# Linear attention and a two-layer feed-forward: the second chunk's attention built like the later chunks' (block transposes, keys in two layouts)

## The chip, the cores and the metric

The kernel runs on one core of one Trainium2 chip. The metric is the device time of one execution in microseconds (us). An execution is compared with others of the same program on the same kind of chip; of the kernel before, three timed runs are shown, and one more execution was recorded by the hardware profiler.

## What is computed

The reference takes q, k and v of shape (8 batches, 8 heads, 576 positions, 64 features). q gets a softmax over its 64 features, k a softmax over the 576 positions. Then k^T v is formed for each head (a 64 x 64 matrix) and q is multiplied by it. The result, 4608 tokens of 512 features, goes through a feed-forward network with 2048 hidden units and a clipped quadratic as its activation.

```python
q_s = np.exp(q - np.max(q, axis=-1, keepdims=True))
q_s = q_s / (np.sum(q_s, axis=-1, keepdims=True) + 1e-09)
k_s = np.exp(k - np.max(k, axis=2, keepdims=True))
k_s = k_s / (np.sum(k_s, axis=2, keepdims=True) + 1e-09)
kv = np.einsum('bhsd,bhse->bhde', k_s, v)
x = np.einsum('bhsd,bhde->bhse', q_s, kv)      # then (tokens, 512)
...
h = x @ w_in
g = np.where(h >= 1, h, np.where(h <= -1, 0.0, (h + 1) ** 2 / 4))
out = g @ w_out
```

All arrays are float32, except the weights, which arrive as 64-bit words.

## The kernel before

**Tiling.** The 4608 tokens are nine chunks of T = 512. The 512 features are four pairs of heads (128 partitions each), the 2048 hidden units 16 blocks f of 128. Chunk 0 starts the kernel; chunks 0, 1 and 2 run the plain feed-forward; chunks 3 to 8 run in couples with fewer products. Every large product is a sum of three products of 128x128 by 128x512 in a reduced float32 format, because each operand is kept as a high and a low part. In the first layer of a plain chunk (`first_layer`, matmuls on line 1352) a block f takes four entries of three matmuls, one for each pair of heads; in the second (`second_layer`, line 1565) it takes four entries of three, one for each slice of 128 tokens. Chunk 0 uses the pairs in the order 0, 2, 1, 3 of the stored weights, so its first two entries of a block need only the first two pairs.

**Weights.** While chunk 0 runs, `weights` turns the 64-bit words into high and low parts: a load of 512 KB (line 496), a scale on ScalarE (503), a shift and a join on VectorE (508, 511), the high part by ScalarE (534), the low part by GpSimd (538). Each block has two halves: half 0 for the first layer, half 1 for the second. The half-0 weights are also stored to DRAM for later chunks (line 567). Four staging tiles (two tags of two) hold the words, so a load waits until an earlier half in its place is finished. Below, "half 1 of block 1" is `weights(1, 1)`.

**Attention, first form** (`attention`, lines 803 to 998, used for chunks 0 and 1 before). For each pair of heads: the keys come transposed (features on partitions, 288 KB), so the maximum over positions is one reduction along a row (853), and the exponential yields the sums (857). Then TensorE transposes the keys back, four blocks of 128 (line 864) and a tail of 64 (line 873), two copies bring them out of PSUM (432, 434), and k^T v is 10 products, which show as 20 matmul records (line 889). For q (256 KB, rows of tokens): maximum, subtract, exponential, sum, reciprocal and multiply, then four TensorE transposes (line 936) and a copy.

**Attention, second form** (`attention_two`, lines 1079 to 1300, used for chunks 2 to 8 before). Two pairs are handled together. The keys come twice, transposed (288 KB, for the maxima alone, line 1116) and in rows of positions (320 KB); v is 325 KB. The maxima are turned by VectorE (1122), stored to DRAM in two pieces and read back spread over all partitions (128 KB, `m_load`); then VectorE subtracts (1143), ScalarE takes the exponential (1149), and k^T v of both pairs is one group of 40 matmul records (line 1159). q comes in a layout of 32 x 32 blocks, so the maximum and the sum are completed with eight small copies and two combinations across blocks (lines 1251 and 1252), and the transpose is one VectorE instruction per pair (line 1287). TensorE does no transposes here.

After either form `x_two` multiplies q by k^T v for two pairs (line 739) and writes the high part (ScalarE, 754) and the low part (VectorE, 761) of x.

**Order.** Each helper above adds entries to a plan; no engine chooses at run time. The list `SEQUENCE` names the entries, by the number in which they were added, in the order in which they are issued, for all engines together; each engine runs its own entries strictly in that order. `SECOND` names the entries that go to their second engine (a copy on VectorE for ScalarE, a square on GpSimd for ScalarE). All DMAs are issued by SyncE (SP) in list order onto one queue. Numbers used below, as the code adds them after the change: 38 to 42 are the x of chunk 0's first two pairs (38 its matmuls, 39 and 41 the high parts, 40 and 42 the low parts), 81 to 85 the same for its other two pairs; 86 to 105 the weights of block 0 half 0, block 1 half 0 and block 0 half 1; 106 to 109 the first layer of block 0; 119 to 125 the half 0 of block 2 (121 its shift, 122 its join); 126 to 131 the half 1 of block 1 (126 its load, 128 its shift, 129 its join); 132 to 135 the first layer of block 1; 110 to 112 the clipping of block 0 (112 its last step, on VectorE); 145 to 151 the half 0 of block 3 (148 its join); 301 to 337 the attention of the second chunk's first two pairs.

Of the kernel before, what the change touches and what calls it, by code (L numbers as in the profile page):

```python
# [18 lines left out]
P = 128  # L19
# [40 lines left out]
KT = 2  # L60


QT, QB = 2, 32
# [32 lines left out]
class Ring:  # L96
# [289 lines left out]
def tile_linear_attention_then_ffn(  # L386
# [416 lines left out]
    def attention(c, pr, due, step, slack):  # L803

        n = f"{c}_{pr}"
        first = c == 0  # L810
        after = 0.0 if first else START
        t = {}
# [1004 lines left out]
```

## Time and profile before

| what | us |
|---|---|
| median of the three timed runs | 833.61 (831.25 to 834.84) |
| the profiled execution, whole | 833.62 |
| its span, first to last instruction | 831.5 |
| TensorE (PE) busy within the span | 821.9 |
| VectorE (DVE) / ScalarE (ACT) / GpSimd (POOL) busy | 511.3 / 400.7 / 298.5 |
| first matmul of the feed-forward (line 1352) starts | 21.09 |
| first matmul of the second layer (line 1565) starts | 29.09 |
| matmul record of line 1352 for chunk 1's first block | 119.00 |

The whole profiled execution is 2.1 us longer than its span. Matmul records overlap one another, since matmuls are pipelined: what a group costs is read from the starts of what stands before and behind it, not from its length. "Waited for" rows name the last thing that an idle engine waited for.

### The profile page before, as it was taken

The page shows a single profiled execution, that of the slowest core. Times are in us where ns is not written, and L with a number is a line of the kernel's source. Part 1 is how long each engine was busy: PE and PEld are TensorE (multiplying, and loading weights), DVE is VectorE, ACT ScalarE, POOL GpSimd, SP SyncE. Part 2 cuts the span into 40 slices and gives each one's busy share as a digit, 9 for nine tenths or more (in the row PEclk, how much of TensorE's full clock was granted, in tenths as well). Part 3 has the DMA queues.
Part 4 walks back from the last instruction along what each step waited for, and adds up shares of the span by engine and source line. Part 5 has one row for each costly group of instructions (what it writes and reads, how often), then busy time and mean ns, then how long its engine had stood idle before and what let it go on. Part 6 is the DMA issues. An engine that isn't in the chain of part 4 may idle for free.

```text
span 831.5 us, 12315 instructions
## 1 busy us (share of the span) xinstructions
PE 821.9 (99%) x4316; PEld 659.2 (79%) x4316; DVE 511.3 (61%) x948; ACT 400.7 (48%) x691; POOL 298.5 (36%) x264
## 2 busy tenths in 40 slices
PE   8999999999999999999999999999999999999998
PEld 6677778877777788877877888787778888788886
DVE  7867688677686867867687546656564144443311
ACT  6877656335365356535455435443453243444521
POOL 4655465453435373311433342323344301111021
PEclk9999999999999999999999999999999999999999
DMA  9897868667687667886867336465564245444232
GB/s 340 276 326 259 311 226 269 211 222 264 222 305 241 210 234 276 277 270 222 302 204 257 115 134 203 152 225 193 177 206 174 76 165 163 141 152 152 76 102 88
DMA packets 70957, 175.05 MB, mean 211 GB/s; under 512 B 8048, under 2 KB 9840, under 8 KB 70896
## 3 DMA queue, kind: packets, MB, share of 16 engines
q1 hardware_dynamic: 70896, 174.27, 62.3%
q8 instruction: 34, 0.56, 0.3%
q14 instruction: 27, 0.22, 0.1%
HBM read 130.71 MB, written 43.53 MB: 210 GB/s over the span
## 4 chain that ended last, share of the span: by engine, by line
PE 92%; DMA 3%; DVE 2%; POOL 1%; issue 1%; ACT 1%; SPq 1%; POOLq 0%; DVEq 0%; ACTq 0%
PE o L1565 45%; PE hA L1411 16%; PE h L1352 14%; PE hC L1411 8%; PE hb L1411 4%; DMA st<-in_w 3%; PE x L739 2%; PE kv L1159 2%; POOL wl L538 1%; SPq L831 1%; PE kv L889 0%; DVE st L508 0%; POOL q L916 0%; DVE st L511 0%; PE tp L936 0%
## 5 line engine op out<-in xcount | busy, mean ns | idle before, releaser
L1565 PE MATMUL o<-wl,gh 128*128 128x512 f32 x576 | 227.2, 394 | 1.0 <-issue 1.0
L1565 PE MATMUL o<-wh,gl 128*128 128x512 f32 x576 | 224.5, 390 | 0.2 <-DVE gl L1554 0.2
L1565 PE MATMUL o<-wh,gh 128*128 128x512 f32 x576 | 224.3, 389 | 0.0
L1411 PE MATMUL hA<-x,w 128*128 128x512 f32 x576 | 143.2, 390 | 0.0
L1508 POOL TENSOR_TENSOR r<-r 128x512 f32<-128x512 f32 x59 | 62.8, 1065 | 221.0 <-ACT r L1502 212.3
L1565 PEld LDWEIGHTS o<-wl,gh 128*128 128x128 f32 x576 | 108.1, 188 | 28.4 <-issue 4.3
L1411 PEld LDWEIGHTS hA<-x,w 128*128 128x128 f32 x576 | 107.8, 188 | 24.4 <-DVE c L1435 1.0
L1565 PEld LDWEIGHTS o<-wh,gl 128*128 128x128 f32 x576 | 108.1, 188 | 23.9 <-DVE gl L1554 1.2
L1565 PEld LDWEIGHTS o<-wh,gh 128*128 128x128 f32 x576 | 108.2, 188 | 21.7
L1352 PE MATMUL h<-x,w 128*128 128x512 f32 x432 | 109.3, 393 | 0.3 <-DVE x L761 0.2
L1352 PEld LDWEIGHTS h<-x,w 128*128 128x128 f32 x432 | 79.9, 188 | 20.1 <-DVE x L761 1.9
L1411 PE MATMUL hC<-x,w 128*128 128x512 f32 x288 | 74.3, 393 | 0.0
L1411 PEld LDWEIGHTS hC<-x,w 128*128 128x128 f32 x288 | 53.4, 188 | 14.2 <-ACT sn_P L432 2.9
L1549 ACT CAST gh<-gs 128x512 fp32r<-128x512 f32 x42 | 26.2, 623 | 78.2 <-PE o L1565 71.2
L1554 POOL TENSOR_TENSOR gl<-gs,gh 128x512 fp32r<-128x512 f32 x22 | 28.4, 1290 | 92.8 <-ACT gh L1549 87.6
L1502 ACT ACTIVATE r<-c,half 128x512 f32<-128x512 f32 x48 | 34.6, 722 | 47.4 <-DVE c L1435 45.8
L1502 ACT ACTIVATE r<-h,half 128x512 f32<-128x512 f32 x48 | 32.9, 688 | 44.6 <-PE h L1352 44.6
L1506 ACT ACTIVATE r<-r 128x512 f32<-128x512 f32 x85 | 53.3, 631 | 1.9
L1260 POOL TENSOR_TENSOR q<-q,qzb 128x512 f32<-128x512 f32 x28 | 32.6, 1182 | 54.1 <-DVE qzb L1282 52.2
L1511 DVE SCALAR_TENSOR_TENSOR h<-h,r 128x512 f32<-128x512 f32 x48 | 33.2, 694 | 28.6 <-ACT r L1506 17.6
L1554 DVE TENSOR_TENSOR gl<-gs,gh 128x512 fp32r<-128x512 f32 x20 | 14.6, 729 | 57.6 <-ACT gh L1549 56.1
L1511 DVE SCALAR_TENSOR_TENSOR c<-c,r 128x512 f32<-128x512 f32 x48 | 34.0, 714 | 12.8 <-ACT r L1506 8.7
(130 smaller groups left out, 1180.0 us busy)
## 6 DMA issues: line engine op xcount, KB each, us to landing
w<-b SPq DMA_DIRECT2D x50, 512.0 KB
w<-s SPq DMA_DIRECT2D x48, 512.0 KB
st<-in_w SPq DMA_DIRECT2D x32, 512.0 KB
g<-c SPq DMA_DIRECT2D x42, 256.0 KB
gs<-g SPq DMA_DIRECT2D x42, 256.0 KB
v<-in_v SPq DMA_DIRECT2D x32, 325.0 KB
q<-in_q SPq DMA_DIRECT2D x36, 256.0 KB
out<-osb SPq DMA_DIRECT2D x35, 256.0 KB
```

Of the source, the lines that this page charges most:

```text
L739: nc.tensor.matmul(t[r][cols, :, p0:p1], kvt[rows, g % NKV, pr, :], q[pr]["tq"][rows, :, p0:p1], start=True, stop=True, tile_position=(r * ...
L1159: nc.tensor.matmul(kv[d, i, :], t[pr]["k"][:, j, d], t[pr]["v"][:, j, e * (D + 1) : (e + 1) * (D + 1)], start=(j == 0), stop=(j == KJ - 1) ...
L1260: nc.gpsimd.tensor_tensor(qf, qf, at, alu)
L1352: nc.tensor.matmul(t["h"], lhs, rhs, start=(turn == 0 and i == 0), stop=(turn == NPAIR - 1 and i == 2),)
L1411: nc.tensor.matmul(banks[b]["h"], lhs, rhs, start=(begins and not kk and not m), stop=(ends and kk == 1 and m == 2), skip_group_check=True,)
L1502: nc.scalar.activation(t["r"], t["h"], AF.Relu, bias=half[:, :1], scale=0.5)
L1506: nc.scalar.activation(t["r"], t["r"], AF.Square)
L1508: nc.gpsimd.tensor_tensor(t["r"], t["r"], t["r"], ALU.mult)
L1511: nc.vector.scalar_tensor_tensor(t["h"], t["h"], 1.0, t["r"], ALU.max, ALU.min)
L1549: nc.scalar.copy(t["gh"], t["h"])
L1554: eng.tensor_tensor(t["gl"], t["h"], f32(t["gh"]), ALU.subtract)
L1565: nc.tensor.matmul(outs[c, j], lhs[:, s], rhs, start=(begins and i == 0), stop=(closes and i == 2),)
```

## The change

Chunk 1 is built by `attention_two` in place of `attention`; `attention` serves chunk 0 alone and loses the branches for other chunks. The host sends the row layout of the keys for one batch more (KT from 2 to 1) and the block layout of q for one chunk more (QT from 2 to 1). The second chunk's two halves take their keys through the "k" tiles. Both lists are new from the first entry to the last: the order of all 3234 entries (3240 before) and the choice of second engines.

```diff
-KT = 2
+KT = 1
-QT, QB = 2, 32
+QT, QB = 1, 32
...
 SEQUENCE = (
...
+    1, 0, 19, 20, 86, 44, 45, 310, 43, 11, 100, 2, 12, 3, 63, 93, 4, 22, 62, 21, 30, 23, 6, 321,
+    5, 31, 322, 7, 24, 25, 119, 8, 64, 26, 88, 313, 54, 27, 32, 55, 13, 33, 87, 14, 56, 15, 34,
+    16, 46, 57, 47, 35, 17, 18, 49, 48, 36, 102, 9, 58, 37, 89, 59, 50, 10, 51, 90, 95, 52, 73,
+    94, 60, 74, 53, 65, 61, 28, 96, 91, 66, 29, 101, 67, 68, 126, 97, 103, 92, 75, 98, 38, 323,
+    69, 76, 104, 77, 145, 120, 70, 301, 78, 324, 71, 99, 39, 121, 79, 72, 303, 128, 80, 105, 40,
+    41, 122, 106, 152, 123, 81, 42, 127, 325, 107, 132, 129, 82, 133, 84, 326, 146, 83, 130,
+    124, 85, 108, 302, 328, 109, 327, 171, 134, 309, 110, 125, 147, 135, 111, 131, 330, 329,
...
-    def attention(c, pr, due, step, slack):
+    def attention(pr, due, step):
...
+        lk = load("kt", kt[0, pr], [P, 1, S], 288)
+        lq = load("q", q[c, pr], [P, NJ, P], 256)
+        lv = load("v", v[c, pr], [P, KJ, P + 2], 325, wait=3.0)
...
-        if not first:
-            rpk.free(kc)
-            tr = do("PE", 0.25, 2.7, kt_tr2, ke, *rpk.wait())
-            tr.mode = 3
-            rk.free(tr)
...
-            tag = ("k", "st1")[h]
+            tag = "st1" if c > 1 and h else "k"
...
-    banks = (ps_a, "b"), (ps_a, "a")
-    one, two = (attend(1, h, START + STEP * (1 + 6 * h), STEP, 1.0, banks) for h in range(2))
-    next(one)
-    at((0, 4), one, two)
+    one, two = (attention_two(1, h, START + 8 + 24 * h, START + 26 + 24 * h) for h in range(2))
+    at((0, 3), one)
+    at((0, 4), one)
+    at((0, 5), two)
     at((0, 6), two)
```

The lines of the list shown are its first seven. In it the loads stand in this order: q and k of pairs 0 and 1, half 0 of block 0 (86), q and v of pair 2, v of the second chunk's pair 0 (310), k of pair 2, half 1 of block 0 (100), v of pair 0, q of pair 3, half 0 of block 1 (93), k of pair 3, v of pair 1, q of the second chunk's pairs 0 and 1 (321, 322), half 0 of block 2 (119), v of pair 3, v of the second chunk's pair 1 (313), half 1 of block 1 (126).

More of the change, by code (lines that the diff above doesn't have):

```diff
@@ L801, in x_two @@
             rxo.free(xdone[c, kk])
-    def attention(c, pr, due, step, slack):
-        n = f"{c}_{pr}"
-        first = c == 0
-        after = 0.0 if first else START
+    def attention(pr, due, step):
+        c, n = 0, f"0_{pr}"
         t = {}
@@ L818, in do @@
             return op(
-                engine, us, at(stage), emit, deps, port=port, slack=slack, after=after, other=other
+                engine, us, at(stage), emit, deps, port=port, other=other
             )
@@ L824, in emit @@
                 size = shape[1] * shape[2]
-                room = KJ * P if name == "k" else VROOM if name == "v" else size
-                if first:
-                    flat = e1.tile([P, room], F32, tag=f"{name}{pr}", name=f"{name}_{n}")
-                else:
-                    flat = ld.tile([P, room], F32, tag=name, name=f"{name}_{n}")
+                room = VROOM if name == "v" else size
+                flat = e1.tile([P, room], F32, tag=f"{name}{pr}", name=f"{name}_{n}")
                 t[name] = flat[:, :size].rearrange("p (j d) -> p j d", j=shape[1])
                 nc.sync.dma_start(t[name].rearrange("p j d -> p (j d)"), src)
-            r = ring(f"ld {name}{first}", NPAIR if first else NLOAD)
-            o = op("SP", 0.45, at(0) - LEAD + wait, emit, r.wait(), kb=kb)
-            r.take(o)
-            return o, r
-        if first:
-            lk, _ = load("kt", kt[0, pr], [P, 1, S], 288)
-            rk = ring("ld kFalse", NLOAD)
-        else:
-            lk, rk = load("k", kt[c, pr], [P, 1, S], 288)
-        lq, rq = load("q", q[c, pr], [P, NJ, P], 256)
-        lv, rv = load("v", v[c, pr], [P, KJ, P + 2], 325, wait=3.0 * first)
-        kpool, ktag = (ps_o, f"o{pr}") if first else (ps_a, "b")
-        rpk, rpq = ring(f"ps {ktag}", 1), ring("ps b", 1)
+            return op("SP", 0.45, at(0) - LEAD + wait, emit, kb=kb)
+        lk = load("kt", kt[0, pr], [P, 1, S], 288)
+        lq = load("q", q[c, pr], [P, NJ, P], 256)
+        lv = load("v", v[c, pr], [P, KJ, P + 2], 325, wait=3.0)
+        rk = ring("ld k", NLOAD)
+        kpool, ktag = ps_o, f"o{pr}"
+        rpk, rpq, rph = ring(f"ps {ktag}", 1), ring("ps b", 1), ring(f"ps h{pr % 2}", 1)
         def kt_max():
-            t["kt"] = t["kt" if first else "k"].rearrange("p j s -> p (j s)")
+            t["kt"] = t["kt"].rearrange("p j s -> p (j s)")
             t["nm"] = sm.tile([P, 1], F32, tag="mc", name=f"nm_{n}", bufs=2)
@@ L864, in kt_tr @@
                 nc.tensor.transpose(t["ep"][:, j, :], t["kt"][:, j * P : (j + 1) * P], ident)
-            if first:
-                kt_tr2()
-            if first and not pr:
+            t["et"] = ps_h.tile([P, T], F32, tag=f"h{pr % 2}", name=f"et_{n}")
+            nc.tensor.transpose(t["et"][:SR, :P], t["kt"][:, NJ * P :], ident)
+            if not pr:
                 more_warm()
-        def kt_tr2():
-            pool, tag = (ps_h, f"h{pr % 2}") if first else (kpool, ktag)
-            t["et"] = pool.tile([P, T], F32, tag=tag, name=f"et_{n}")
-            nc.tensor.transpose(t["et"][:SR, :P], t["kt"][:, NJ * P :], ident)
         def kt_copy(engine):
@@ L951, in attention @@
         rrz.take(kz)
-        et = ring(f"ps h{pr % 2}", 1) if first else rpk
-        tr = do("PE", 0.6, 2, kt_tr, ke, *rpk.wait(), *(et.wait() * first))
+        tr = do("PE", 0.6, 2, kt_tr, ke, *rpk.wait(), *rph.wait())
         tr.mode = 3
@@ L958, in attention @@
         rk.take(kc)
-        if not first:
-            rpk.free(kc)
-            tr = do("PE", 0.25, 2.7, kt_tr2, ke, *rpk.wait())
-            tr.mode = 3
-            rk.free(tr)
-        et.take(tr)
+        rph.take(tr)
         kd = do("DVE", 0.25, 2.8, kt_tail, tr, kc, other=copies[1])
-        et.free(kd)
-        deps = [kc, kd, lv, *(rpk.wait() if not first else [])]
-        mm = do("PE", 0.9, 3.5, kv_mm, *deps)
+        rph.free(kd)
+        mm = do("PE", 0.9, 3.5, kv_mm, kc, kd, lv)
         mm.mode = 2
-        if not first:
-            rpk.take(mm)
         rk.free(mm)
@@ L976, in attention @@
         rrz.free(kf)
-        rv.free(mm)
         qm = do("DVE", 0.68, 0.5, q_max, lq, *rqm.wait())
@@ L990, in attention @@
         rpq.take(tr)
-        rq.free(tr)
-        if first:
-            early_users.extend((mm, tr))
+        early_users.extend((mm, tr))
         rt = ring(f"wk t{'ab'[pr % 2]}", 2)
@@ L998, in attention, with attend @@
         return t, qc
-    def attend(c, h, due, step, slack, banks):
+    def attend(h, due, step):
         two = 2 * h, 2 * h + 1
-        made_ = {pr: attention(c, pr, due + 3 * step * (pr % 2) * (c > 0) + 2.0 * (pr % 2) * (not c), step, slack) for pr in two}
-        yield
-        at = due + step * 4.6 + 3 * step * (c > 0) + 2.0 * (not c)
-        q = {pr: made_[pr][0] for pr in two}
-        x_two(c, h, at, q, [made_[pr][1] for pr in two], banks, START if c else 0.0)
-        yield
+        made_ = [attention(pr, due + 2.0 * (pr % 2), step) for pr in two]
+        banks = [(ps_o, f"o{pr}") for pr in two]
+        q = {pr: m[0] for pr, m in zip(two, made_)}
+        x_two(0, h, due + step * 4.6 + 2.0, q, [m[1] for m in made_], banks, 0.0)
     def x_sums(c, kk, due):
@@ L1106, in emit @@
                 nc.sync.dma_start(t[pr][name].rearrange("p j d -> p (j d)"), src)
-            r = ring(tag, NST) if tag == "st1" else ring(f"ld {tag}False", NLOAD)
+            r = ring(tag, NST) if tag == "st1" else ring(f"ld {tag}", NLOAD)
             o = op("SP", 0.45, due - LEAD, emit, r.wait(), kb=kb)
@@ L1641, in tile_linear_attention_then_ffn @@
     for h in range(2):
-        banks = [(ps_o, f"o{2 * h + r}") for r in range(2)]
-        for _ in attend(0, h, 4.0 * h, 1.5, 0.0, banks):
-            pass
+        attend(h, 4.0 * h, 1.5)
     halves = sorted((f + 1.5 * part, f, part) for f in range(NF) for part in range(2))
```

430 rows, old and new, of tables (SECOND, SEQUENCE) are left out of this document.

## The prediction

> **What bounds the kernel now.** The page comes first: the span, the busy line of TensorE (PE) and its row in the 40 slices.
>
> ```profile
> span 831.5 us, 12315 instructions
> ...
> PE 821.9 (99%) x4316; PEld 659.2 (79%) x4316; DVE 511.3 (61%) x948; ACT 400.7 (48%) x691; POOL 298.5 (36%) x264
> ...
> PE   8999999999999999999999999999999999999998
> ...
> DMA  9897868667687667886867336465564245444232
> ```
>
> TensorE is idle for 831.5 - 821.9 = 9.6 us in all, and the slices put that at the two ends. The table of stretches says where exactly.
>
> ```profile
> 120.00:160.00 40.00, 40.00 (x211) 32.80 (x209) 32.92 (x59) 19.12 (x33) 25.06 (x23) 1.00 0.70 221
> ...
> 700.00:800.00 100.00, 100.00 (x437) 81.40 (x436) 38.32 (x57) 43.13 (x71) 10.65 (x10) 1.00 0.39 130
> 800.00:832.00 32.00, 27.40 (x121) 22.34 (x120) 4.48 (x7) 5.98 (x10) 7.72 (x6) 1.00 0.27 89
> ```
>
> The first number behind the length is PE's busy time, and the rows left out read the same: from 120 us on PE is never idle until the tail. So a microsecond of work taken from PE is a microsecond of time, and a wait counts only in the first 120 us or in the tail. The waits of PE after its start are few:
>
> ```profile
> PE o L1565 <- issue: 1.0, 1, 1.0
> PE tp L936 <- DVE kvt L717: 0.7, 1, 0.7
> PE et L873 <- ACT k L432: 0.5, 1, 0.5
> ...
> PE o L1565 <- DVE gl L1554: 0.2, 1, 0.2
> ```
>
> **PE work that goes.** Costs are read from starts in PE's timeline.
>
> ```profile
> 34.13 0.39 PE L1565 MATMUL o<-wh,gl 128*128 128x512 f32 x1
> 34.45 0.95 PE L889 MATMUL kv<-v,k 128*64 128x65 f32 x20
> ...
> 35.66 0.39 PE L1565 MATMUL o<-wh,gh 128*128 128x512 f32 x1
> ...
> 72.26 0.39 PE L1565 MATMUL o<-wh,gl 128*128 128x512 f32 x1
> 72.49 0.60 PE L936 MATMUL tp<-ident,q 128*128 128x128 f32 x4
> ...
> 73.16 0.40 PE L1565 MATMUL o<-wh,gh 128*128 128x512 f32 x1
> ...
> 96.44 0.39 PE L1565 MATMUL o<-wh,gl 128*128 128x512 f32 x1
> 96.68 0.27 PE L873 MATMUL et<-ident,k 128*64 128x128 f32 x1
> ...
> 97.02 0.39 PE L1565 MATMUL o<-wh,gh 128*128 128x512 f32 x1
> ...
> 135.50 5.60 PE L1352 MATMUL h<-x,w 128*128 128x512 f32 x24
> 140.94 0.39 PE L1565 MATMUL o<-wl,gh 128*128 128x512 f32 x1
> ...
> 157.94 2.20 PE L1352 MATMUL h<-x,w 128*128 128x512 f32 x9
> 160.08 1.39 PE L1159 MATMUL kv<-v,k 128*64 128x65 f32 x40
> ...
> 161.73 0.39 PE L1565 MATMUL o<-wh,gh 128*128 128x512 f32 x1
> ```
>
> The rows at 135.50 and 140.94 give the pace of ordinary matmuls: 24 in 5.44 us, 0.227 each. Four transposes of q: 73.16 - 72.26 = 0.90, less the two matmuls in it, 0.45. The four of k are the same operation on the same shape, so 0.45 too. With four pairs that is 8 x 0.45 = 3.6 us. The tail's transpose: 0.58 - 0.45 = 0.13, four times 0.5. The k^T v of one pair in the old form: 1.53 - 0.45 = 1.08, four times 4.3; of two pairs in the new form: 3.79 less ten matmuls, 2.27, is 1.52, twice 3.0. That saves 1.3. In all 5.4 us go; one group of 0.45 stands at 26.8 us, ahead of the wait of 1.0 for the first second-layer matmul, and shortens nothing there. **PE term: -4.9 us.** The x products of the chunk are the same.
>
> **Waits that go.** The waits of 0.7 (a transpose of q behind VectorE) and 0.5 (the tail's transpose behind a copy) belong to instructions that vanish: **-1.2 us**. What is late next is unknown. Two k^T v groups and the x groups remain that can wait; the new form has more steps in front of them (store and reload of the maxima). I take **+0.5 us**, one wait of the size seen, with bounds 0 and 3.
>
> **The start.** The new list changes the order of the first 25 us, and this is where I expect most of the gain to be lost. In VectorE's part of it the low part of x for chunk 0's first pair (entry 40) stands behind the shift of half 1 of block 1 (128), which cannot run before that half has landed; and its load (126) is the 21st.
>
> ```profile
> 12.24 1.13 DVE L508 TENSOR_SCALAR st<-st 128x512 uint32<-128x512 uint32 x1 [0.34 <-DMA st<-in_w]
> ...
> 20.64 0.68 DVE L511 SCALAR_TENSOR_TENSOR st<-sg,st 128x512 uint32<-128x512 uint32 x1
> ...
> 21.09 0.97 PE L1352 MATMUL h<-x,w 128*128 128x512 f32 x3
> 21.23 0.41 DVE L508 TENSOR_SCALAR st<-st 128x512 uint32<-128x512 uint32 x1
> ...
> 24.59 1.66 PE L1352 MATMUL h<-x,w 128*128 128x512 f32 x6
> ...
> 29.09 0.47 PE L1565 MATMUL o<-wl,gh 128*128 128x512 f32 x1 [1.01 <-issue]
> ```
>
> ```profile
> 10.00:12.00 2.00, 1.26 (x9) 0.92 (x9) 1.80 (x6) 2.00 (x6) 1.53 (x2) 1.00 1.02 344
> 12.00:14.00 2.00, 2.00 (x31) 1.70 (x29) 1.76 (x3) 1.92 (x5) 1.04 (x1) 1.00 1.05 411
> ```
>
> The last two columns are the DMA engines' busy share and GB/s: they are full. Before, half 0 of block 0 was the tenth load, behind 4 k, 3 q and 2 v: 1152 + 768 + 650 + 512 = 3082 KB, and VectorE got it at 12.24. In the new list the 21st load ends at 6 q + 4 k + 6 v + 5 halves = 1536 + 1152 + 1950 + 2560 = 7198 KB. The 4116 KB between are 4.21 MB: at 411 GB/s 10.3 us, so it lands at 22.5; at 344 GB/s at 24.5. I take 22.5, the rate of the row that is nearer in time and kind. Then shift 0.41, low part 0.68 (the join's length; both read and write 128x512): the first matmul of the feed-forward starts at about 23.7, against 21.09.
>
> By the Trainium skill, "DMA: Bandwidth & Descriptors", section "Where 436 GB/s comes from", transfers from HBM are bound near 358 GB/s for a core; by that the load would land at 24.0 and the sum be 1.5 us worse. This trace moved 411 GB/s, so the measurement decides.
>
> Behind it stand on VectorE, before both low parts of the other two pairs are done: a join, a low part, the combination of q's maxima (four copies and one small operation), a join and two low parts.
>
> ```profile
> L1251 DVE COPY qmo<-qa 32x32 f32<-32x32 f32 x56 | 13.2, 236 | 1.0
> ```
>
> That is five times 0.68, four copies of 0.236 and some 0.2: 4.5 us after 23.6, so 28.1. The fourth and last entry of block 0 starts then; before it was the second of the six-matmul row, 24.59 + 0.68 = 25.3, and the second layer came 3.8 later, at 29.09. The same 3.8 gives 31.9; a join of another half now stands ahead of the clipping on VectorE (148 ahead of 112), which I count once, 0.7: 32.6. **Start term: +3.5 us**; bounds +1.5 (the other operations close up) and +5.5 (344 GB/s).
>
> **The tail.** In the new list the left half of the last slice's output is copied and stored behind the copy of slice 1, which waits for the last matmul; before, it was ahead. One more half copy, **+0.4 us** (bounds 0 and 1):
>
> ```profile
> 825.40 0.37 ACT L432 COPY osb<-o 128x256 f32<-128x256 f32 x1 [3.00 <-PE o L1565]
> ```
>
> **Vector work and bytes.** VectorE gets four subtractions on the keys and sixteen small copies for the row statistics (4 x 1.02 + 16 x 0.24 = 8 us, the largest items) and gives up copies. The queue gets four more key loads of 320 KB and two reloads of maxima of 128 KB, 1.57 MB.
>
> ```profile
> 29.00:106.00 77.00, 75.49 (x413) 58.79 (x414) 56.62 (x108) 56.29 (x101) 43.96 (x36) 1.00 0.87 292
> ...
> L1143 DVE TENSOR_TENSOR k<-k,m 128x640 f32<-128x640 f32 x24 | 24.1, 1018 | 2.0 <-DMA m<-mk 2.0
> ...
> DVE st L508 <- DMA st<-in_w: 13.9, 11, 2.0
> ```
>
> VectorE is busy 57 of 77 us there, so 8 more fit. I cost both at nothing, since PE waited only 0.2 us for anything behind the weights in that stretch, though VectorE waited 13.9 us for their words. If the cover is gone it is the second rival.
>
> **Sum.** -4.9 - 1.2 + 0.5 + 3.5 + 0.4 = -1.7 us. The profiled execution took 833.62 and the median is 833.61, so the forecast is **831.9 us** for either.
>
> **Rivals.** First, **the start does not move**: loads land earlier, or the wait hides behind attention work that PE has to do anyway. Then the start term is 0: 831.9 - 3.5 = 828.4. For it: PE is idle for several us before 21 us in any order, and the list must suit some model of the queue. Against: the bytes and the order on VectorE are written in the list. Chance 0.20.
>
> Second, **DMA becomes the bound of chunk 0**, the other side. The queue is busy 0.87 of 29 to 106 us at 292 GB/s, 336 GB/s when busy; 1.57 MB is 4.7 us. If the weights' words have no slack left, each of these delays the join, the low part and then PE: 831.9 - 0.5 + 4.7 = 836.1. It decides where VectorE's waits for words pass on to PE; the store and reload of the maxima also stand in SP's list ahead of word loads (that of half 1 of block 4), which then queue behind a wait for VectorE. For it: 13.9 us of such waits already. Against: 10 us of the 77 are free, and part of the bytes are moved to the start, where I have counted them. Chance 0.22.
>
> Third, **the slow clock returns**. The same 18 small matmuls at the start:
>
> ```profile
> 1.36 4.21 PE L1748 MATMUL warm<-ident 128*128 128x128 f32 x18 [1.36 <-POOL ident masks.py:199]
> ...
> 6.11 2.17 PE L1748 MATMUL warm<-ident 128*128 128x128 f32 x18
> ```
>
> The first group takes 4.21 us, the second 2.17: PE starts at half its pace. My times leave PE gaps of 2 to 3 us ahead of 23.7 and of 32.6. A gap that lost the pace again would cost about as much again, 4.21 - 2.17 = 2.0: 833.9. Chance 0.08. The Trainium skill, "TensorE: Matmul & The Clock Gate", Part 1, has this rule: the clock falls to half after an idle window of about 3.4 us. By it gaps of 2 to 3 us would do no harm; the longest wait seen before, 1.36, did none that shows.
>
> **Chances and range.** Forecast 0.50, the rivals 0.20, 0.22 and 0.08. A measurement of this kernel tells about 0.5% (4.2 us) from no change: faster means below 829.4, slower above 837.8. Faster gets the first rival nearly whole and the low edge of the forecast's spread, 0.22; slower the upper part of the second (it needs 1.7 us more) and a start beyond its bound, 0.14; same 0.64. The range runs from the first rival to the second with the unknown waits on top: 828.0 to 837.2.
>
> **What would show it.** Right: no records on lines 864, 873 and 936 behind 25 us; 40 records on line 1159 in two more groups; the first row on line 1352 at 23 to 25 us, the first on line 1565 at 32 to 34; PE busy throughout from 120 us. Wrong: a first row on line 1565 near 29 (first rival); idle time of PE between 35 and 120 us over 3 us with DMA at 0.95 or more (second); matmul starts 0.45 apart in a row behind a gap (third). If the busy time of PE falls by less than 4 us, the PE term is mis-sized.

## The result, and the profile after

| | median us | range | runs |
|---|---|---|---|
| before | 833.37 | 831.25 to 834.84 | 4 |
| after | 838.38 | 837.88 to 838.92 | 4 |

The ratio is 1.0062, with a 95% interval of 1.0048 to 1.0077: 0.6% slower, clear of the noise, outside the range of the forecast and on the other side of it. The profiled execution of the changed kernel took 838.3 us. Its page:

```profile
span 836.5 us, 12240 instructions
...
PE 819.2 (98%) x4280; PEld 660.3 (79%) x4280; DVE 524.7 (63%) x974; ACT 405.0 (48%) x690; POOL 280.7 (34%) x245
...
PE   6799999999999999999999999999999999999997
...
PEclk9899999999999999999999999999999999999999
...
DMA  8788996668586786857777535465555344444232
```

The span grew by 5.0 us while TensorE's busy time fell by 2.7. The slices put the loss into the first two, some 40 us; and there the row of the granted clock has an 8. The change takes out 31 lines ahead of the matmuls, so line 1321 is the first layer (1352 before), 1534 the second (1565), 1128 the new k^T v (1159), 919 the q transposes (936). TensorE's timeline at the places that the prediction named:

```profile
14.08 1.12 PE L919 MATMUL tp<-ident,q 128*128 128x128 f32 x4 [4.21 <-POOL q L899]
...
28.28 1.65 PE L1321 MATMUL h<-x,w 128*128 128x512 f32 x3 [1.66 <-DVE x L760]
...
39.83 0.47 PE L1534 MATMUL o<-wl,gh 128*128 128x512 f32 x1 [1.72 <-ACT gh L1518]
...
41.60 4.39 PE L1321 MATMUL h<-x,w 128*128 128x512 f32 x12
```

The first row of the feed-forward starts at 28.28 (21.09 before), the first of the second layer at 39.83 (29.09). TensorE has done the same 24 first-layer matmuls ahead of the latter in both kernels, so the span can be cut there: up to it **+10.7 us**, behind it 836.5 - 39.83 = 796.7 against 831.5 - 29.09 = 802.4, **-5.7 us**. The whole loss lies ahead of the second layer's start, or in the slow stretch right behind it.

The stretches of 2 us show the second thing. The first number behind the length is PE's busy time; the last three are granted clock, DMA share and GB/s.

```profile
14.00:16.00 2.00, 1.92 (x9) 1.73 (x10) 1.05 (x3) 0.61 (x2) 1.03 (x2) 0.51 1.00 366
...
20.00:22.00 2.00, 1.44 (x25) 1.06 (x24) 1.79 (x5) 1.69 (x5) 1.81 (x2) 1.00 0.15 52
...
28.00:30.00 2.00, 1.72 (x7) 0.97 (x11) 1.94 (x6) 1.14 (x2) 0.00 (x0) 0.50 0.86 244
30.00:32.00 2.00, 2.00 (x9) 0.39 (x10) 0.97 (x3) 0.12 (x2) 1.51 (x2) 0.50 1.04 413
...
42.00:44.00 2.00, 2.00 (x6) 1.59 (x5) 1.97 (x4) 1.54 (x3) 0.79 (x1) 0.50 0.78 263
```

Behind TensorE's three longest waits (4.21, 1.66 and 1.72 us in the rows above) the clock was halved: 12 matmuls took 4.39 us at 41.60, where they take 2.89 at full pace (e6 below, the same place in the program). And the queue was nearly empty at 20 to 22 us (0.15), just where the prediction had it full until the load of half 1 of block 1. That load went out only at 21.84, as SyncE's queue shows:

```profile
21.84 0.33 SPq L495 DMA_DIRECT2D st<-in_w  x1
```

It needs a staging tile, and the earliest half in these tiles was finished by GpSimd's low part (line 537) at 20.51 + 1.30 = 21.81. That low part stands behind seven of GpSimd's eight steps for the q of the four pairs, of which these rows show the last two; the third row is the low part:

```profile
17.04 1.04 POOL L899 TENSOR_TENSOR q<-q,qrz 128x512 f32<-128x512 f32 x1 [2.01 <-DVE qrz L914]
19.51 1.04 POOL L899 TENSOR_TENSOR q<-q,qm 128x512 f32<-128x512 f32 x1 [1.43 <-DVE qm L894]
20.51 1.30 POOL L537 TENSOR_TENSOR w<-st,w 128x512 fp32r<-128x512 f32 x1
```

The waits of SyncE's queue in the first 40 us name the same step as the longest:

```profile
SPq L495 <- POOL w L537: 11.2, 2, 6.2
```

VectorE then meets its shift and the low part of x just as the prediction had it, only 4 us later, and with a shift of 1.20 us for 0.41:

```profile
26.43 1.20 DVE L507 TENSOR_SCALAR st<-st 128x512 uint32<-128x512 uint32 x1 [0.24 <-DMA st<-in_w]
27.55 0.68 DVE L760 TENSOR_TENSOR x<-x,x 128x512 fp32r<-128x512 f32 x1
```

**Two theories** follow. *Clock*: TensorE's gaps bring the half clock back, and that is the 5 us. *Order*: the new list starts the feed-forward late, whatever the clock, and that is the 5 us. A third, *form*: the new attention itself costs more. The experiments part them.

### The profile page after: what moved, and what is told of

Its sections match the earlier page's. It is cut to its first block, busy times and chain, and to the rows that moved or that the text cites. A ratio compares the mean times of both kernels' runs of the same rounds, so it can differ in the third digit from the quotient of the medians.

```text
span 836.5 us, 12240 instructions
## 1 busy us (share of the span) xinstructions
PE 819.2 (98%) x4280; PEld 660.3 (79%) x4280; DVE 524.7 (63%) x974; ACT 405.0 (48%) x690; POOL 280.7 (34%) x245
## 4 chain that ended last, share of the span: by engine, by line
PE 91%; issue 3%; POOL 2%; DMA 2%; DVE 2%; ACT 1%; DVEq 0%; POOLq 0%; ACTq 0%
PE o L1534 45%; PE hA L1380 16%; PE h L1321 13%; PE hC L1380 8%; PE hb L1380 4%; PE kv L1128 2%; PE x L738 2%; DMA st<-in_w 2%; POOL wl L537 1%; POOL q L1229 0%; DMA q<-in_q 0%; PE tp L919 0%; POOL w L537 0%; PE ep L852 0%; DVE st L507 0%
## 5 line engine op out<-in xcount | busy, mean ns | idle before, releaser
L1477 POOL TENSOR_TENSOR r<-r 128x512 f32<-128x512 f32 x51 | 54.3, 1068 | 219.7 <-ACT r L1471 219.7
L1321 PEld LDWEIGHTS h<-x,w 128*128 128x128 f32 x432 | 82.2, 192 | 23.3 <-DVE x L760 1.9
L1523 DVE TENSOR_TENSOR gl<-gs,gh 128x512 fp32r<-128x512 f32 x29 | 22.7, 784 | 67.6 <-ACT gh L1518 67.6
L1475 ACT ACTIVATE r<-r 128x512 f32<-128x512 f32 x93 | 58.1, 631 | 2.2
L1229 POOL TENSOR_TENSOR q<-q,qmb 128x512 f32<-128x512 f32 x32 | 34.4, 1091 | 71.4 <-DVE qmb L1221 54.5
L1229 POOL TENSOR_TENSOR q<-q,qzb 128x512 f32<-128x512 f32 x32 | 35.7, 1130 | 58.9 <-DVE qzb L1251 43.2
L1480 DVE SCALAR_TENSOR_TENSOR c<-c,r 128x512 f32<-128x512 f32 x48 | 37.0, 778 | 8.6 <-POOL r L1477 6.2
```

The source lines that it names most:

```text
L1229: nc.gpsimd.tensor_tensor(qf, qf, at, alu)
L1321: nc.tensor.matmul(t["h"], lhs, rhs, start=(turn == 0 and i == 0), stop=(turn == NPAIR - 1 and i == 2),)
L1475: nc.scalar.activation(t["r"], t["r"], AF.Square)
L1477: nc.gpsimd.tensor_tensor(t["r"], t["r"], t["r"], ALU.mult)
L1480: nc.vector.scalar_tensor_tensor(t["h"], t["h"], 1.0, t["r"], ALU.max, ALU.min)
L1523: eng.tensor_tensor(t["gl"], t["h"], f32(t["gh"]), ALU.subtract)
```

## The experiments

Each kernel's median stands against runs of the kernel before on the same chip. "Rest" is the span of the profiled run less the start of the first second-layer matmul; the clock is the mean granted in that run.

| run | ratio to before | 95% interval | second layer starts | rest | clock |
|---|---|---|---|---|---|
| before | | | 29.09 | 802.4 | 1.000 |
| after | 1.0062 | 1.0048 to 1.0077 | 39.83 | 796.7 | 0.992 |
| e1 | 1.0047 | 1.0032 to 1.0061 | 37.22 | 796.5 | 0.997 |
| e2 | 1.0034 | 1.0019 to 1.0050 | 35.29 | 798.8 | 0.998 |
| e3 | 1.0047 | 1.0029 to 1.0064 | 37.41 | 797.6 | 0.996 |
| e4 | 1.0046 | 1.0029 to 1.0063 | 29.25 | 804.7 | 1.000 |
| e5 | 1.0147 | 1.0120 to 1.0173 | 29.00 | 813.1 | 0.996 |
| e6 | 1.0003 | 0.9990 to 1.0015 | 35.96 | 796.0 | 0.999 |
| e7 | 1.0093 | 1.0073 to 1.0113 | 36.90 | 800.8 | 0.991 |
| e8 | 1.0037 | 1.0024 to 1.0050 | 38.02 | 797.0 | 0.997 |
| e9 | 1.0030 | 1.0018 to 1.0042 | 37.86 | 796.0 | 0.999 |
| e10 | 1.0097 | 1.0082 to 1.0111 | 41.04 | 796.1 | 0.993 |
| e11 | 1.0034 | 1.0022 to 1.0046 | 34.32 | 799.8 | 1.000 |
| e12 | 1.0032 | 1.0020 to 1.0044 | 34.41 | 800.1 | 0.999 |
| e13 | 1.0021 | 1.0013 to 1.0030 | 33.74 | 798.5 | 0.999 |

### The clock alone: small matmuls in the gaps (e1, e2, e6)

The kernel after with more of the 128x128 matmuls that it already uses at its start (each shows as two records), in the gaps where TensorE only waits. Nothing of the list is touched. e1 fills the first gap, behind pair 1's key transposes:

```diff
-            if not pr:
-                more_warm()
+            if pr < 2:
+                more_warm((WARM, 16)[pr])
```

> Sixteen more of the small warm-up matmuls are issued behind the key transposes of chunk 0's second pair, so that PE is not idle from 9.9 to 14.1 us; all else as in the changed kernel. If the idle time costs through the clock: the granted clock reads 1.0 from 14 to 18 us (0.51 and 0.63 there now), the first row of line 1321 comes about 1 us earlier than 28.3, the later halved stretches stay, and the time is about 837 against 838.4. If the order on the queues alone sets the start: no change, 838.0 to 838.8.

e2 fills the second too, behind the last q transposes, and was to fill the third, ahead of the second layer:

```diff
+            if pr == 3:
+                more_warm(7, ps_h.tile([P, P], F32, tag="h0", name="warm_h"))
...
+                    if not c and not j:
+                        more_warm(7, outs[c, j][:, :P])
```

> As before it, and seven more small matmuls each behind the last transposes of q in chunk 0 and ahead of the first second-layer matmul, so that PE's three long waits of the first 40 us are filled; no wait is shortened by itself. If the clock is the cause of most of the loss: granted clock 1.0 throughout, 6.2 us of work at half pace from 28.3 and 3.5 us from 41.3 run at full pace, minus 3.1 and minus 1.7 us and up to 1 us from the first stretch: 832.5 to 834. If the order alone sets the start: 838.0 to 839.

The list runs slice 1 of the second layer first, so e2's third group stood behind the gap and not in it. e6 puts it there:

```diff
-                    if not c and not j:
+                    if not c and j == 1:
```

> The changed kernel with the three fillings of the second run, the third now ahead of the first second-layer matmul in the list's order (there it stood ahead of the third, where PE was busy). If the clock is the cause of most of the loss: clock 1.0 up to 46 us, the filling costs nothing and the halved stretch at 36 to 41 us goes, 3 us less than the 836.2 of that run, 832.5 to 833.5. If not: 836.

Measured: 836.03 (835.01 to 838.59, 6 runs), 836.16 (834.49 to 837.42, 6 runs) and 833.78 us (832.59 to 834.44, 10 runs). e1 alone takes 2.6 us off the second layer's start (37.22): its first row comes at 27.00, as expected, and of the later halved stretches only one is left, from 27.30 to 30.71, where all were expected to stay. e2's timeline shows the one halved stretch it has left, behind a gap of 1.72 us, and e6's the same places at full pace:

```profile
35.29 0.47 PE L1538 MATMUL o<-wl,gh 128*128 128x512 f32 x1 [1.72 <-ACT gh L1520]
...
36.46 0.63 PE L1538 MATMUL o<-wl,gh 128*128 128x512 f32 x1
```

```profile
27.29 0.94 PE L1323 MATMUL h<-x,w 128*128 128x512 f32 x3 [0.21 <-DVE x L760]
...
34.07 1.72 PE L1720 MATMUL o<-ident 128*128 128x128 f32 x14
35.96 0.47 PE L1538 MATMUL o<-wl,gh 128*128 128x512 f32 x1 [0.17 <-ACT gh L1520]
...
37.62 2.89 PE L1323 MATMUL h<-x,w 128*128 128x512 f32 x12
```

The clock is shown to cost the difference of the ratios, 1.0062 - 1.0003 = 0.0059, or **4.9 us** (from 3.3 to 6.5, an estimate from the two intervals; by the spans 836.5 - 832.0 = 4.5). With it gone the changed kernel takes what the kernel before takes; no gain is left over. So the clock theory accounts for the loss against before, but not for the gain that did not come: the second layer still starts 35.96 - 29.09 = 6.9 us later, at full pace.

### Order or form (e4, e5, e7)

e4 is the kernel after with the first 218 entries of its list, all up to the second layer's second block, in the order and on the engines that they had before (the new attention's own entries where those of the old stood):

```diff
 SEQUENCE = (
-    1, 0, 19, 20, 86, 44, 45, 310, 43, 11, 100, 2, 12, 3, 63, 93, 4, 22, 62, 21, 30, 23, 6, 321,
...
+    0, 19, 1, 20, 44, 2, 43, 62, 21, 3, 86, 63, 4, 22, 321, 45, 11, 23, 6, 64, 30, 12, 93, 7, 25,
...
```

> The second chunk in its new form, but the first 218 entries of the list (up to the second layer of block 1) in the order and on the engines of the kernel before, with the new form's entries at the places of the old ones'. If the loss lies in the new order of the start: the first row of line 1534 at 29 to 30 us, granted clock 1.0 throughout, and the gain of the vanished transposes and waits shows, 5 to 6 us: 827.5 to 829. If the new form itself (its bytes, its work on VectorE) costs what it saves: 833 or more.

Measured: 836.49 us (835.37 to 838.21, 4 runs). The start is back, 29.25 us, and the clock of the profiled run is full: **the new form does not need the late start**. But the rest is 804.7, 8 us more than with the list of after. The stretches and waits show where it went:

```profile
20.00:40.00 20.00, 16.38 (x68) 10.91 (x65) 16.73 (x33) 14.35 (x26) 10.13 (x9) 1.00 0.77 242
40.00:60.00 20.00, 15.06 (x62) 10.88 (x60) 13.42 (x28) 11.76 (x21) 9.87 (x9) 1.00 0.90 302
60.00:80.00 20.00, 18.40 (x111) 14.26 (x112) 17.24 (x34) 14.60 (x26) 10.27 (x8) 1.00 0.87 299
```

```profile
PE o L1522 <- ACT gh L1506: 4.2, 2, 2.6
PE o L1522 <- POOL wl L525: 1.6, 1, 1.6
PE h L1309 <- DVE gl L1511: 1.5, 2, 1.0
```

TensorE stands 10.2 us between 20 and 80, behind clipped values and weights that are late, with VectorE busy 47 of the 60 and DMA at 0.90 or less: no engine is full. That their entries come in the wrong order is an argument from these rows; e4 does not exclude that the new form's extra work on VectorE costs something behind the start.

e5 carries this on: the whole list of before, with the new attention's entries set in by hand, and its k^T v in the other PSUM bank so that the two do not wait for each other:

```diff
-            b["kv"] = kv = ps_a.tile([P, 2, D + 1], F32, tag="a", name=f"kv_{n}")
+            b["kv"] = kv = ps_a.tile([P, 2, D + 1], F32, tag="b" if c == 1 else "a", name=f"kv_{n}")
...
-            ra = ring("ps a", 1)
+            ra = ring("ps b" if c == 1 else "ps a", 1)
```

> The second chunk in its new form, its k^T v in another PSUM bank (b for a), and the whole list in the order and on the engines of the kernel before, with the new form's entries set by hand among them near the old ones' places. If the new form as such gains what the prediction's first two terms say, 4.9 + 1.2 us, and only the new list loses it: first row of line 1534 near 29, clock 1.0, about 828 to 830 where the kernel before has 833. If its bytes and its work on VectorE take it back: 833 or more, with PE idle for over 5 us between 30 and 110 us.

Measured: 845.51 us (843.84 to 848.48, 4 runs); start 29.00, rest 813.1. A hand-made order for the new form loses 11 us behind an early start, in the same kinds of waits (3.3 for the clipping, 3.1 for a low part of a weight). It says nothing of the form itself. Two stretches at half clock lie in it (37.69 to 41.11 and 102.55 to 105.96), which can hold up to 3.4 of the 11 us.

e7 is the other half: the kernel **before**, old form, with chunk 0's entries of the start in the new order. Chunk 0's loads have tiles of their own, so their wait for an earlier user is left out:

```diff
-            o = op("SP", 0.45, at(0) - LEAD + wait, emit, r.wait(), kb=kb)
+            o = op("SP", 0.45, at(0) - LEAD + wait, emit, [] if first else r.wait(), kb=kb)
...
 SEQUENCE = (
-    0, 19, 1, 20, 44, 2, 43, 62, 21, 3, 126, 63, 4, 22, 87, 45, 11, 23, 6, 64, 30, 12, 133, 7,
...
+    1, 0, 19, 20, 126, 44, 45, 43, 11, 140, 2, 12, 3, 63, 133, 4, 22, 62, 21, 87, 30, 23, 6, 5, 31,
...
```

> The kernel before, with chunk 0's entries of the first 218 of the new list in the new order and on the new engines; the second chunk keeps its old form and all else its old order. If the start's order alone costs what the changed kernel's start shows (10.7 us up to the first row of line 1565), of which the waits that it removes later give back some: 838 to 844. If the order costs only beside the new form's loads and reductions: 833 to 835.

Measured: 841.79 us (839.47 to 842.41, 4 runs).

```profile
13.94 1.12 PE L923 MATMUL tp<-ident,q 128*128 128x128 f32 x4 [4.22 <-POOL q L903]
...
28.32 0.96 PE L1339 MATMUL h<-x,w 128*128 128x512 f32 x3 [0.23 <-DVE x L748]
...
36.90 0.47 PE L1552 MATMUL o<-wl,gh 128*128 128x512 f32 x1 [1.07 <-ACT gh L1536]
```

The same wait of 4.2 us and the same late start, without the new form: the start order is the cause of both. Behind that wait the clock was halved for 13.65 us:

```profile
13.11:26.76 13.65, 12.07 (x96) 8.41 (x98) 8.53 (x24) 8.13 (x17) 7.06 (x7) 0.50 0.80 283
```

So the 0.93% that this start costs the old kernel is order and clock together, and e7 does not part them. The new form and the later part of the list, on that start, bring the rest from 800.8 to 796.7: most of the gain that was forecast is there, though which of the two brings it is not shown.

### Which entry makes the start late (e3, e8, e9, e10)

e3 takes the prediction's suspect out: the shift (128) of half 1 of block 1, with its scale, join and high part and the scale of half 0 of block 3, go behind the four low parts of x. No fillers.

```diff
-    303, 128, 80, 105, 40, 41, 122, 106, 152, 123, 81, 42, 127, 325, 107, 132, 129, 82, 133,
-    84, 326, 146, 83, 130, 124, 85, 108,
+    303, 80, 105, 40, 41, 122, 106, 152, 123, 81, 42, 325, 107, 132, 82, 133, 84, 326, 83, 124,
+    85, 127, 128, 129, 130, 146, 108,
```

> Only the list: the scale, shift, join and high part of half 1 of block 1 (and the scale of block 3 behind them) move behind the last low part of chunk 0's x, so that this low part no longer waits for a load. If that wait was the start's bound, as the prediction had it: the first row of line 1321 at 26.6 to 27 us instead of 28.3, and the time 1.5 us less, 836.9. If the clock's halved stretches hold the loss: the start moves by as much but the stretch behind it stays halved, 836.5 to 838. If the start is bound by something else (the low part by GpSimd of block 0, the transposes of q): no change.

Measured: 836.34 us (835.46 to 838.68, 4 runs). The feed-forward starts at 26.23, 2 us sooner, somewhat more than expected of the suspect, so that wait did bound the first row. But the second layer, at 37.41, waits 4.2 us for the clipping, and two stretches are halved (13.25 to 16.66, 37.14 to 40.56), so the time does not part the two theories.

e8 is e3 with the fillers of e6:

> The fillers of the run before keep the clock; in addition the shift, scale, join and high part of half 1 of block 1 and the scale of half 0 of block 3 stand behind the four low parts of x. If the start is late because VectorE waits at that shift, the first row of the feed-forward comes at 25.5 to 26.5 (27.29 with fillers alone), the first second-layer row at 34.5 to 35.5 (35.96), and the time is 832.5 to 833.3. Rival: the second layer is held by something else on VectorE and ScalarE (with the late shift alone it waited 4.2 us for the clipping): the second-layer row stays at 36 and the time at 833.8.

e9 is e8 with the join, high and low part of half 0 of block 0 brought forward, and the load (126) behind them:

```diff
-    34, 16, 46, 57, 47, 35, 17,
+    34, 89, 16, 46, 57, 47, 90, 35, 91, 126, 17,
```

> As the run before, and the join, the high and the low part of half 0 of block 0 come forward (the low part on GpSimd ahead of pair 2's and pair 3's q), so that the load of half 1 of block 1 can go out at 16 to 17 us in place of 20.9. If the queue of loads is what made the start late, every later load lands some 4 us earlier and the second layer starts at 33 to 34.5: 831.3 to 832.5. Rival: ScalarE and VectorE are what the start waits for, then the second layer stays where the run before has it, within 0.5 us.

e10 is e9 with pairs 0 and 1's q steps ahead of pair 2's, and 5 fillers for 16 in the first gap:

```diff
-    7, 24, 25, 119, 8, 64, 26, 88, 313, 54, 27, 32, 55, 13, 33, 87, 14, 56, 15, 34, 89, 16, 46,
-    57, 47, 90, 35, 91,
+    7, 13, 32, 87, 24, 25, 119, 8, 64, 26, 88, 14, 33, 313, 54, 15, 34, 16, 35, 55, 56, 89, 27,
+    46, 57, 47, 90, 91,
...
-                more_warm((WARM, 16)[pr])
+                more_warm((WARM, 5)[pr])
```

> As the run before, and pair 0's and pair 1's q steps (exponential, sum, reciprocal, multiply) stand ahead of pair 2's subtraction; the first filler group is cut from 16 matmuls to 5. The first transposes of q start at about 11 us (14.09). If the wait of 4.2 us there is what the changed order pays, the first feed-forward row comes at 23.5 to 25, the second layer at 31.5 to 33.5, and the time is 829.5 to 831.5, below the kernel before. Rival: the weights' words bound the start, or the time won is given back in waits between 30 and 80 us as when the start had the old order: 832 to 834.

Measured: 835.99 (834.81 to 839.07, 6 runs), 835.69 (834.88 to 836.77, 5 runs) and 840.98 us (838.83 to 841.98, 4 runs). **No start came as hoped, and of the rivals only e9's came true**: its second layer stayed within 0.5 us of e8's (37.86 and 38.02). In e9 the load went out at 17.25 in place of some 21: the load was late, but it was not what the second layer waited for. The fillers blur the first row in both: the low part of x was ready at 25.75 in e8 and 25.99 in e9, but seven fillers held TensorE, and the row came at 27.20 and 27.44. That can hold some 1.4 us of the second layer's start, not the whole miss. e8 shows, TensorE first and then ScalarE, what the second layer waited for:

```profile
34.05 1.72 PE L1708 MATMUL o<-ident 128*128 128x128 f32 x14
38.02 0.76 PE L1526 MATMUL o<-wl,gh 128*128 128x512 f32 x1 [2.25 <-ACT gh L1508]
...
33.34 0.66 ACT L521 CAST wh<-st 128x512 fp32r<-128x512 f32 x1 [2.41 <-DVE st L498]
```

The moved high part of half 1 of block 1 now stands on ScalarE ahead of the clipping, and waits there 2.41 us for its join. In e10 pair 2's exponential waited for its subtraction behind the two multiplies on GpSimd, the key steps of pair 2 queued behind it on ScalarE, and TensorE stood 2.92 us a little later:

```profile
12.28 0.66 PE L907 MATMUL tp<-ident,q 128*128 128x128 f32 x4 [1.68 <-POOL q L887]
15.86 1.11 PE L840 MATMUL ep<-ident,kt 128*128 128x128 f32 x4 [2.92 <-ACT kt L833]
```

Five fillers were too few besides: the clock was halved from 13.36 on.

```profile
13.36:23.60 10.24, 7.00 (x69) 5.76 (x69) 5.97 (x13) 4.73 (x11) 4.45 (x4) 0.50 0.94 342
```

TensorE was busy for 7.0 us of that stretch, so up to 3.5 us (an estimate: half of it) may be the clock's; its first row, at 30.63, lies 3.2 us behind e9's. e10 is no test of that order at full pace. In these runs each move that took a wait away put its neighbours behind another; no single entry was found to be the cause of the late start.

### Can both be had? (e11, e12, e13)

e11 is e6 with all low parts of x ahead of that half's shift and of q's maxima, and block 0's clipping ahead of that half's high part and the second chunk's exponentials; 2 fillers for 7 in the second gap:

```diff
-    303, 128, 80, 105, 40, 41, 122, 106, 152, 123, 81, 42, 127, 325, 107, 132, 129, 82, 133,
-    84, 326, 146, 83, 130, 124, 85, 108, 302, 328, 109, 327, 171, 134, 309, 110, 125, 147, 135,
-    111, 131, 330, 329, 148, 112, 178, 149, 113, 150, 331, 153, 114, 136,
+    303, 80, 105, 40, 41, 122, 106, 152, 123, 81, 42, 128, 127, 107, 132, 82, 133, 84, 83, 124,
+    85, 325, 326, 327, 129, 108, 302, 109, 171, 134, 309, 110, 125, 147, 135, 111, 112, 146,
+    113, 328, 130, 131, 148, 114, 330, 329, 149, 178, 150, 331, 153, 136,
```

> From the traces of the last three runs: the second layer is held by ScalarE and VectorE, whose lists put the high part and scale of other halves and the second chunk's q ahead of the clipping of block 0. Here all four low parts of x come before the shift and join of half 1 of block 1 and before the combination of q's maxima, and the clipping of block 0 comes before that half's high part and the second chunk's exponentials; the second filler is cut from 7 matmuls to 2. If the order on these two engines alone sets the start, the first feed-forward row comes at 25.5 to 26.3 (27.29 with fillers alone), the first second-layer row at 33 to 34.5 (35.96), the rest behind it takes 796 as in every run with the changed list, and the time is 831.0 to 832.5. Rival: the weights' words and the staging tiles bind, and what was put back is then waited for between 35 and 80 us: second layer early, rest 798 or more, time 833.5 or above.

e12 is e11 with pair 3's steps and the high parts of x earlier:

```diff
-    29, 101, 67, 68, 126, 97, 103, 92, 75, 98, 38, 323, 69, 76, 104, 77, 145, 120, 70, 301, 78,
-    324, 71, 99, 39, 121, 79, 72, 303, 80, 105, 40, 41, 122, 106, 152, 123, 81, 42, 128,
+    29, 75, 101, 67, 68, 126, 69, 97, 76, 70, 77, 103, 92, 78, 98, 38, 39, 41, 104, 145, 120,
+    301, 71, 99, 40, 42, 121, 79, 72, 303, 80, 105, 122, 323, 324, 106, 152, 123, 81, 128,
```

> As the run before, and pair 3's q and k steps stand ahead of the joins and low parts of the first weights, the high parts of x of pairs 0 and 1 right behind their matmuls, the block maxima of the second chunk's q behind the low parts. If order alone sets the start: first feed-forward row at 24 to 25, second layer at 31.5 to 33, rest 796, time 829.5 to 831. Rival as before: rest 798 or more, time 832 or above.

e13 is e12 with block 1's clipping (138 to 140) ahead of the combination of q's sums (332):

```diff
-    154, 306, 155, 158, 307, 173, 156, 151, 159, 138, 172, 160, 332, 139, 161, 157, 140, 115,
+    154, 138, 155, 139, 140, 332, 306, 158, 307, 173, 156, 151, 159, 172, 160, 161, 157, 115,
```

> As the run before, and the clipping of block 1 stands ahead of the join and high part of half 1 of block 2, of the second chunk's sums of q across blocks, and of the shift of block 4. In the run before the last step of that clipping began at 41.9 us behind those sums (1.70 us), and TensorE stood 2.33 us. If such places in the hand-made list alone gave the earlier start back, the wait of 2.33 goes, the rest behind the first second-layer row is 797.5 to 798.5 in place of 800.1, and the time is 833.0 to 834.3, about that of the kernel before. Rival: the weights are what is late; the wait moves on to the next block, the rest stays at 799.5 or more, and the time at 835 or above.

Measured: 835.88 (835.02 to 836.40, 5 runs), 835.72 (834.38 to 836.74, 6 runs) and 834.87 us (833.97 to 836.81, 12 runs). e11 and e12 start the second layer some 1.6 us before e6, as the first theory had it for e11, and then need 799.8 and 800.1 behind it: the rivals' numbers came true, but the longest wait is not for weights or staging tiles, which they named. e12's VectorE shows the place, four small copies that took 1.70 us ahead of the last step of the clipping of block 1, and TensorE the wait for it:

```profile
40.06 1.70 DVE L1210 COPY qzo<-qs 32x32 f32<-32x32 f32 x4
41.80 0.19 DVE L1211 TENSOR_TENSOR qzb<-qs,qzo 128x32 f32<-128x32 f32 x1
41.91 0.68 DVE L1513 TENSOR_TENSOR gl<-h,gh 128x512 fp32r<-128x512 f32 x1
```

```profile
42.64 2.33 PE L1311 MATMUL h<-x,x 128*128 128x512 f32 x9 [2.32 <-DVE gl L1513]
```

e13 takes that wait away and gains 1.6 us behind the start (798.5), with three waits still there:

```profile
33.74 0.47 PE L1526 MATMUL o<-wl,gh 128*128 128x512 f32 x1 [0.75 <-ACT gh L1508]
46.96 0.50 PE L1526 MATMUL o<-wh,gl 128*128 128x512 f32 x1 [1.04 <-DVE gl L1513]
...
72.47 1.65 PE L1311 MATMUL h<-x,w 128*128 128x512 f32 x6 [1.03 <-DVE gl L1513]
```

The rest fell into the band that the order theory gave, the median lies between the two theories' times. So the order is part of what gives the time back; whether a list exists that starts at 29 and still has a rest of 796 was not found, and stays open. No version tried beats the kernel before; e6 equals it and beats the kernel after.

## Why the prediction was wrong

**The PE term was about right.** Forecast 5.4 us of work less in all. The changed kernel's own busy time fell by 2.7 only, less than the 4 that the prediction named as the sign of a wrong size, but it holds the halved stretches. e4 has the same work at a clock of 1.000 throughout, and its TensorE is busy 816.8 us against 821.9: 5.1. Behind the second layer's start, where 4.9 were forecast, the busy time is 796.89 before, 791.94 in e4 and 790.72 in e6: 5.0 and 6.2. The k^T v of line 1128 has 560 records for 480, two more groups of 40.

**The waits and the tail were about right.** Behind the second layer's start the terms make -4.9 - 1.2 + 0.5 + 0.4 = -5.2; the trace has -5.7, although a halved stretch lies in it, and e6, at full pace, 796.0 - 802.4 = -6.4. One wait of 1.0 for a clipped low part came in (forecast 0.5). From the last matmul's end to the end it is 4.3 us for 4.1: +0.2 for +0.4.

**The start term is the step that failed:** "+3.5 us; bounds +1.5 and +5.5", measured +10.7. Two things were wrong in it, the time at which one load lands and a clock taken as full.

*Order, +6.9* (e6, at full pace). The prediction let the load of half 1 of block 1 land "at 22.5", by the bytes in front of it in a full queue. The queue was not full: at 20 to 22 us its share was 0.15, since SyncE itself waited, for a staging tile that GpSimd had not finished. The front of this document tells of that wait, and the sum did not follow it to GpSimd's list, where the low part stands behind the q of the pairs. At full pace the whole miss lies there: the first row came at 27.29 for 23.7 forecast, and from it to the second layer e6 took 8.7 us for 8.9 forecast. But moving that load alone does not bring the start back: with it at 17.25 (e9) the second layer came at 37.86, and with the shift out of the way and the clipping early (e11) at 34.32, still 5.2 us late. One chain with a landing time was the wrong model of 25 us in which four engines run in a new order. What else holds the start, entry by entry, stays open.

*Clock, +3.9 of the 10.7 and part of what follows; 4.9 in all.* This was the third rival, with a chance of 0.08 and a price of 2.0. Its mechanism was right, its price and its chance were not. The price counted one halved stretch of some length; there were four of 3.41 us (14.05 to 17.47, two from 27.71 to 34.53, 41.36 to 44.77). The sign that the prediction named was there: from 31.78 to 33.22 three matmuls started 0.48 apart. The chance leaned on the rule of the Trainium skill, "TensorE: Matmul & The Clock Gate", Part 1, that an idle window of about 3.4 us brings the half clock: the prediction read it as a gap of 3.4 us. Here stretches behind gaps of 1.7 us were halved; the measurement decides. The same section says that the window runs freely, which the prediction did not use, and with it the runs in the last section agree. The chance's other support, a wait of 1.36 us that did no harm, says nothing: that wait stands ahead of the very first matmul, whose group ran at half pace anyway (4.21 us for 2.17).

**The forecast's sum was not a sum of independent terms.** At full clock an earlier second layer goes with a longer rest: 29.25 and 804.7, 33.74 and 798.5, 35.96 and 796.0. These runs fit one reading: up to 80 us the order of VectorE, ScalarE and GpSimd sets the time, and a later start, up to some 36 us, only moves TensorE's idle time to the front (beyond it, in e9 and e10, the rest stays at 796). It is a reading of these lists, not shown. In the changed kernel what was won behind the start was paid ahead of it, and the clock made the loss.

**The other rivals.** The start did move (first rival). DMA is not the bound of chunk 0 (second): in the changed kernel TensorE waited 1.0 us in all between 42 and 130 us, for a clipped low part, and in the stretch of its late start the queue ran empty.

## What to carry to other kernels

When a list of many queues is new, its start is read by following each load back to what frees its buffer, on the engine that frees it; bytes and a rate give only the earliest landing. Where TensorE has gaps near 2 us at its start, put small matmuls into them before anything else is tuned: here that was worth 4.9 us, as much as the change takes out of TensorE's work. Too many of them hold the next real matmul up, as in e8 and e9. And before a late start is counted as a loss, or an early one as a gain, look at what the other engines still have to finish behind it.

## What the hardware showed that was not expected

The length of a gap alone does not say whether the half clock comes. Gaps of 1.72 us (after, at 39.83) and 2.25 (e8, at 38.02) were followed by it; gaps of 1.72 (e1, at 37.22), 1.87 (e9) and 2.33 (e11, at 42.56) were not. The times at which the clock changes say more. In the changed kernel it fell at 14.05, 27.71 and 41.36 us and rose at 17.47, 34.53 and 44.77: all these times lie whole multiples of 3.41 us apart. So do e3's two falls (13.25 and 37.14, seven times 3.41), and the halved stretches of e10 and e7 are three and four times as long. Another execution has other times, but the same spacing. So the clock is set window by window, in windows of 3.41 us that run on their own, and a gap counts by how much of one window it fills. The rows cut the traces at these windows, counted on from a change of the clock in the same run; the first four are of the changed kernel, the fifth of e8, the sixth of e1, the rest of e9. The last row is TensorE's after e9's gap of 1.87 us, which is split between the two windows above it:

```profile
14.05:17.47 3.42, 3.39 (x21) 2.87 (x23) 2.33 (x8) 0.88 (x3) 1.41 (x2) 0.50 1.03 386
27.71:34.53 6.82, 6.25 (x18) 3.31 (x19) 5.16 (x13) 3.81 (x8) 3.61 (x4) 0.50 0.88 306
37.95:41.36 3.41, 1.69 (x7) 1.06 (x7) 2.89 (x6) 3.38 (x7) 1.31 (x1) 1.00 0.63 226
41.36:44.77 3.41, 3.41 (x10) 2.64 (x9) 3.25 (x7) 1.87 (x4) 1.30 (x1) 0.50 0.89 265
...
34.59:38.00 3.41, 1.18 (x11) 1.00 (x10) 2.62 (x5) 3.38 (x7) 1.39 (x2) 1.00 0.80 252
...
34.13:37.54 3.41, 1.69 (x9) 1.09 (x7) 3.07 (x6) 3.33 (x6) 0.87 (x1) 1.00 0.92 259
...
33.61:37.03 3.42, 2.39 (x18) 2.08 (x16) 2.58 (x6) 3.39 (x7) 1.38 (x1) 1.00 0.72 216
37.03:40.44 3.41, 2.58 (x10) 1.91 (x11) 3.02 (x7) 2.47 (x5) 1.30 (x1) 1.00 0.79 250
...
37.86 0.47 PE L1526 MATMUL o<-wl,gh 128*128 128x512 f32 x1 [1.87 <-ACT gh L1508]
```

The clock fell behind windows in which TensorE was busy for 1.18 us (e8) and 1.69 (after, from 37.95), and it stayed behind windows with 1.69 (e1), 2.39 and 2.58 (e9). The border lies near half a window; that 1.69 is on both sides says that busy time in these traces does not fix it exactly. What brings the full clock back is not read from busy time either: after a window with 3.02 it rose (e3, from 13.25), after one with 3.41 it did not (e7, from 19.94).

The four copies of 32x32 took 1.70 us in e12, where the row of before gives 0.236 each, 0.94. The trace has 1.14 us for one of them and 0.17 for the others. The long one ended at 41.20, 0.03 us behind an operation of GpSimd on 128x512 (39.87 to 41.17); that it waited for it is likely, and no run tests it.
